# Loading the first keys in two parts, 16 rows ahead of the first query weights and 112 rows behind them

## The chip, the cores and the metric

The kernel runs on one core of a Trainium2 chip. The metric is the device time of one execution in microseconds; lower is better. All times are of the same kernel program on the chip, and the time before is the median of three runs.

## What is computed

A decode step for 4 tokens of width 448: a layer norm, attention of 16 query heads over 8 key/value heads with the last 1024 positions of a cache (head width 256), an output projection with a residual, then a second block of layer norm, a dense layer of 1792 with GELU, and a dense layer back with a residual.

```python
B, Sq, D = 4, 1, 448;  Hq, Hkv, Sk, Dh = 16, 8, 4096, 256;  W = 1024
def A(x):      # x is already normed
    q = (x @ wq).reshape(B, Sq, Hq, Dh).transpose(0, 2, 1, 3)
    k = repeat(k_cache[:, :, Sk - W:], 2, axis=1); v = repeat(v_cache[:, :, Sk - W:], 2, axis=1)
    p = softmax(einsum("bhqd,bhkd->bhqk", q, k) * Dh ** -0.5)
    return einsum("bhqk,bhkd->bhqd", p, v).transpose(0, 2, 1, 3).reshape(B, Sq, Hq * Dh) @ wo
h = x + A(layernorm(x))
y = layernorm(layernorm(h))
out = h + gelu(y @ w1 + b1) @ w2 + b2
```

Everything is in float32. Some 88 MB have to be read, nearly all of it keys, values and weights that are used once.

## The kernel before, in words

The work is cut by key/value head, two heads to a stage. For each stage the queries of both heads come from `wq` (tile `pq`), the scores (`b_s`) from the keys, the softmax and a transpose give `pT`, and the values (`b_o`) and the output weights (`b_acc`) end the stage. At the end stands the dense block with `w1` and `w2`.

All loads are issued from SyncE (SP) on one queue, in the order of the code. They go into a ring of three large slots in SBUF (`slot(...)`, all called `slot` in the profile). The helper `load(t, at, src)` issues one DMA of 128 rows (one row for each of the 128 partitions) into columns of a slot, and `cut` names the parts. Keys, values and weights of neighbouring stages are laid out behind one another on the host, so that one DMA brings a mixture of them: the arrays `l1` to `l8`. A load waits on SP until the last reader of its slot is done; the first three slots need no such wait.

The first slot `t0` takes two loads. `wq0` has 1828 columns: the query weights of head 0 (`WEIGHTS`, 1792 columns), and x and the two bias vectors in column form (`COLUMNS`, 36 columns). `k0` has 9728 columns: the keys of head 0 (8192 columns) and three quarters of the query weights of head 1 (1536 columns). The last part of head 1's query weights comes in two small loads of 32 rows each into `wq1_last`. Then follow `l1`, `l2` and the rest.

On the engines, the layer norm of x comes first (`column_mean` on PE, which reads `xT` out of `wq0`), then the projection of head 0, then six transposes that spread x and the biases (`b_t<-ident,slot`); the projection of head 1 and the scores of head 0 wait for `k0`.

Each operation is recorded first; a wait is derived for each from the part of a tile that it reads or writes (`Machine._needs`, in granules of 4 partitions), and every DMA has a semaphore of its own, which is called `landed_` and a number. So a reader of a part that two DMAs wrote waits for both. All instructions carry line 75, that of the recording helper.

Of the kernel before, what the change touches and what calls it, by code (L numbers as in the profile page):

```python
# [24 lines left out]
HALF = CACHE // 2  # L25
WEIGHTS = 4 * D
SLOT = CACHE + 2 * WEIGHTS + HALF
COLUMNS = ND * B + 4 + 4 * 4
# [172 lines left out]
def block_kernel(nc, wq0, k0, wq1, l1, l2, l3, l4, l5, l6, l7, l8, k7, vo, v7, wo, w1, w2, out):  # L201
    real, nc = nc, Machine(nc)
# [18 lines left out]
    def slot(name):  # L221
        return ring.tile([P, SLOT], F32, tag="slot", name=name)

    def load(t, at, src, pieces=None):
        dst = t[:, at : at + src.shape[-1]]
        at = 0
        for n in pieces or (src.shape[-1],):
            nc.sync.dma_start(dst[:, at : at + n], src[:, at : at + n])
            at += n
        return dst  # L230

    def cut(t, sizes):
        parts, at = [], 0
        for n in sizes:
            parts.append(t[:, at : at + n])
            at += n
        return parts


    def wq_parts(y, t, last=None):  # L240
        parts = [(a, y[:, a, :], slice(0, 512), t[:, a * 512 : (a + 1) * 512]) for a in range(3)]
        if last is not None:
            return parts + [(3, y[:H, 3, :], slice(0, 512), last)]
        for i in range(2):
            parts.append((3, y[:, 3 + i, :], slice(i * 2 * P, (i + 1) * 2 * P), t[:, 3 * 512 :]))
        return parts
# [204 lines left out]


    t = slot("t0")
    wqt, xT, b2T, b1T = cut(load(t, 0, wq0), (WEIGHTS, ND * B, 4, 4 * 4))
    wqt = wq_parts(yT[0], wqt)
    xT = xT.rearrange("p (a b) -> p a b", a=ND)
    ka, kb, wqt1 = cut(load(t, WEIGHTS + COLUMNS, k0), (HALF, HALF, 3 * 512))
    for i in range(2):
        nc.sync.dma_start(
            wq1_last[i * Q : (i + 1) * Q, :], wq1[i].rearrange("e (p c) -> e p c", c=512)[:, :4, :]  # L460
# [44 lines left out]
    ka, kb, va = cut(load(slot("l1"), 0, l1), (HALF, HALF, HALF))  # L505
# [14 lines left out]
    wq_a, wq_b, ka, kb, k2 = cut(load(slot("l3"), 0, l3), (WEIGHTS, WEIGHTS, HALF, HALF, HALF))  # L520
# [16 lines left out]
    v, wo_a, wo_b, ka = cut(load(slot("l5"), 0, l5), (CACHE, WEIGHTS, WEIGHTS, HALF))  # L537
# [6 lines left out]
    kb, ka, k2 = cut(load(slot("l6"), 0, l6), (HALF, HALF, HALF))  # L544
# [14 lines left out]
    vb, wo_a, wo_b, ka, kb = cut(load(slot("l8"), 0, l8), (HALF, WEIGHTS, WEIGHTS, HALF, HALF))  # L559
# [249 lines left out]
```

## Time and profile before

| | us |
|---|---|
| median of 3 runs | 211.96 (211.85 to 212.13) |
| profiled execution, its own time | 211.87 |
| span from the first to the last instruction in it | 210.6 |
| PE busy | 139.0 |
| DVE busy | 28.8 |
| ACT busy | 14.4 |

The profiled execution lies 0.09 us below the median; 1.27 us of it lie outside the span. The DMA queue of SP moved 88.30 MB in 3392 packets. "SPq" in the profile's rows is the time that SP's queue takes to issue a DMA, not the transfer itself; "us to landing" is from the issue until all of its data is in place. A row that has `<-DMA slot<-k` in its brackets waited for a load of keys.

### The profile page before, as it was taken

The numbers are of one execution on the slowest core, as the hardware profiler recorded it, in microseconds if no ns is written. First come the engines' busy times: TensorE is split into PE (matmuls) and PEld (weight loads), VectorE is DVE, ScalarE is ACT, GpSimd is POOL, SyncE is SP. The second block draws the span as 40 slices with busy tenths as digits, with TensorE's granted clock in tenths as the row PEclk, the third lists the DMA queues.
The fourth block names the chain that finished last, engine by engine and source line by source line (L and its number), as shares of the span: only waits on it lengthen the run. The fifth ranks groups of instructions, "written<-read, shape, count | busy, mean of one in ns | idle before, by whom it ended". The sixth has DMA issues, their size and how long they took to land.

```text
span 210.6 us, 2206 instructions
## 1 busy us (share of the span) xinstructions
PE 139.0 (66%) x984; PEld 47.2 (22%) x984; DVE 28.8 (14%) x135; ACT 14.4 (7%) x34; POOL 5.0 (2%) x17
## 2 busy tenths in 40 slices
PE   0467759621971679198359775419806999888996
PEld 0420202200220223034012222102301233224332
DVE  7210101300020011013001104000100213012320
ACT  2010000200000010020000002000100002010311
POOL 5100000000000000000000000000000000000100
PEclk9999996996799559969967999757965899999999
DMA  7999999899999999999999999999999999999993
GB/s 296 429 399 473 448 492 389 386 436 507 398 398 410 531 389 410 410 519 398 413 411 448 481 398 425 434 470 398 434 411 442 416 428 429 425 407 439 424 409 138
DMA packets 3400, 88.42 MB, mean 420 GB/s; under 512 B 512, under 2 KB 768, under 8 KB 1344
## 3 DMA queue, kind: packets, MB, share of 16 engines
q1 hardware_dynamic: 3392, 88.30, 97.6%
q8 instruction: 7, 0.11, 0.2%
q14 instruction: 1, 0.01, 0.0%
HBM read 88.23 MB, written 0.07 MB: 419 GB/s over the span
## 4 chain that ended last, share of the span: by engine, by line
DMA 77%; PE 18%; SPq 2%; DVE 1%; issue 1%; ACT 0%
DMA slot<-l 64%; DMA slot<-w 14%; PE b_o L75 9%; PE b_s L75 4%; PE b_acc L75 3%; SPq L75 2%; PE b_m L75 1%; DVE oT L75 1%; DVE w_o L75 0%; PE b_t L75 0%; DVE o_u L75 0%; ACT o_u L75 0%; DVE o_res L75 0%
## 5 line engine op out<-in xcount | busy, mean ns | idle before, releaser
L75 PE MATMUL b_o<-slot,pT 128*32 128x512 f32 x224 | 33.6, 752 | 29.3 <-DMA slot<-l 28.5
L75 PE MATMUL b_s<-slot,qT 128*32 128x512 f32 x256 | 36.6, 722 | 10.4 <-DMA slot<-l 9.1
L75 PE MATMUL b_m<-slot,yT 128*32 128x512 f32 (+1 forms) x76 | 11.9, 734 | 11.5 <-DMA slot<-l 6.4
L75 PEld LDWEIGHTS b_o<-slot,pT 128*32 128x32 f32 x224 | 7.8, 132 | 51.4 <-DMA slot<-l 30.9
L75 PE MATMUL b_t<-idle 128*32 128x512 bf16 x64 | 18.1, 404 | 0.5 <-DVE pT L75 0.5
L75 PEld LDWEIGHTS b_s<-slot,qT 128*32 128x32 f32 x256 | 8.8, 128 | 35.9 <-issue 22.5
L75 ACT ACTIVATE o_p<-b_s,w_nm 128x512 f32<-128x512 f32 x8 | 5.4, 682 | 93.1 <-DVE w_nm L75 93.1
L75 DVE TENSOR_REDUCE w_mx<-b_s 128x1 f32<-128x512 f32 x8 | 5.5, 692 | 43.7 <-PE b_s L75 43.7
L75 DVE TENSOR_SCALAR w_o<-b_o,w_rec 128x512 f32<-128x512 f32 x4 | 3.0, 751 | 52.5 <-PE b_o L75 52.5
L75 PEld LDWEIGHTS b_m<-slot,yT 128*32 128x32 f32 x76 | 4.3, 142 | 17.9 <-DMA slot<-l 6.9
L75 PEld LDWEIGHTS b_t<-idle 128*32 128x32 bf16 x64 | 5.9, 100 | 10.3 <-issue 5.8
L75 DVE TENSOR_REDUCE w_sm<-b_m 128x32 f32<-128x128 f32 x4 | 1.2, 291 | 48.2 <-PE b_m L75 48.2
L75 PE MATMUL b_t<-ident,o_p 128*128 128x128 f32 x32 | 5.0, 285 | 4.0 <-ACT o_p L75 3.9
L75 PE MATMUL b_acc<-slot,oT 128*32 128x448 f32 x52 | 6.1, 545 | 1.9 <-DVE oT L75 1.9
L75 ACT COPY w_qs<-b_m 128x512 f32<-128x512 f32 x4 | 2.3, 584 | 60.8 <-PE b_m L75 60.8
L75 POOL TENSOR_TENSOR o_r<-w_ve,mhalf 128x1 f32<-128x1 f32 x2 | 1.1, 542 | 189.0 <-DVE w_ve L75 189.0
L75 PE MATMUL b_m<-ident,w_qs 128*128 128x128 f32 x16 | 3.5, 361 | 2.9 <-ACT w_qs L75 2.9
L75 PEld LDWEIGHTS b_t<-ident,o_p 128*128 128x128 f32 x32 | 3.4, 141 | 7.4 <-ACT o_p L75 7.4
L75 PE MATMUL b_m<-slot,mean 128*128 128x12 f32 (+1 forms) x4 | 1.1, 370 | 5.6 <-DMA slot<-wq 5.6
L75 PE MATMUL b_o<-slot,yT 128*32 128x512 f32 x10 | 4.6, 594 | 0.0
L75 PE MATMUL b_m<-ident,w_o 128*128 128x128 f32 x20 | 3.3, 286 | 1.8 <-DVE w_o L75 1.8
L75 DVE COPY pT<-b_t 128x16 f32<-128x16 f32 x32 | 3.3, 167 | 6.0 <-PE b_t L75 6.0
(94 smaller groups left out, 66.7 us busy)
## 6 DMA issues: line engine op xcount, KB each, us to landing
slot<-l SPq DMA_DIRECT2D x6, 7936.0 KB, 43.0
slot<-l SPq DMA_DIRECT2D x2, 6144.0 KB, 34.1
slot<-k SPq DMA_DIRECT2D x1, 4864.0 KB, 15.9
slot<-vo SPq DMA_DIRECT2D x1, 4544.0 KB, 33.1
slot<-k SPq DMA_DIRECT2D x1, 4096.0 KB, 43.5
slot<-v SPq DMA_DIRECT2D x1, 3072.0 KB, 19.0
slot<-w SPq DMA_DIRECT2D x1, 2240.0 KB, 28.6
slot<-w SPq DMA_DIRECT2D x1, 1792.0 KB, 34.0
```

What stands on the lines that cost most here:

```text
L75: self.machine.add(Op(self.name, lambda: getattr(issuer, what)(*args, **kwargs), outs, ins, what))
```

## The change

`k0` is no longer loaded as one DMA of 128 rows. Its first 16 rows (partitions 0 to 15, 38,912 bytes each) are issued as the very first DMA, ahead of `wq0`; the other 112 rows (partitions 16 to 127) follow behind `wq0`. The places of the data in the slot, the number of bytes, and all the work on the other engines stay as they were.

```diff
     t = slot("t0")
+    k0t = t[:, WEIGHTS + COLUMNS :][:, : k0.shape[-1]]
+    nc.sync.dma_start(k0t[:16], k0[:16])
     wqt, xT, b2T, b1T = cut(load(t, 0, wq0), (WEIGHTS, ND * B, 4, 4 * 4))
     wqt = wq_parts(yT[0], wqt)
     xT = xT.rearrange("p (a b) -> p a b", a=ND)
-    ka, kb, wqt1 = cut(load(t, WEIGHTS + COLUMNS, k0), (HALF, HALF, 3 * 512))
+    nc.sync.dma_start(k0t[16:], k0[16:])
+    ka, kb, wqt1 = cut(k0t, (HALF, HALF, 3 * 512))
     for i in range(2):
         nc.sync.dma_start(
             wq1_last[i * Q : (i + 1) * Q, :], wq1[i].rearrange("e (p c) -> e p c", c=512)[:, :4, :]
```

SP's queue begins like this before. `slot<-wq` is `wq0`, `slot<-k` the first keys `k0`, `wq_last` the small loads of head 1's last query weights, `slot<-l` the mixed loads `l1`, `l2` and on:

```order
L75 DMA slot<-wq 128x1828
L75 DMA slot<-k 128x9728
L75 DMA wq_last<-wq 32x1x512 x2
L75 DMA slot<-l 128x12288
L75 DMA slot<-l 128x15872 x4
```

And after:

```order
L75 DMA slot<-k 16x9728
L75 DMA slot<-wq 128x1828
L75 DMA slot<-k 112x9728
L75 DMA wq_last<-wq 32x1x512 x2
L75 DMA slot<-l 128x12288
```

The first 16 rows of the keys have moved to the head of the queue, and everything else stands one issue later.

On PE, whose instructions keep their order, the waits of the projection of head 1 change. Before, `landed_27` is all of `k0`, and 28 and 29 are the two loads of `wq_last`; after, 26 is the 16 rows, 28 the 112 rows, and 29 and 30 `wq_last`:

```order
-L75 MATMUL b_m<-slot,yT 32x512 [waits landed_27]
+L75 MATMUL b_m<-slot,yT 32x512 [waits landed_26,landed_28]
 L75 MATMUL b_m<-slot,yT 32x512 x2
-L75 MATMUL b_m<-wq_last,yT 32x512 [waits landed_28,landed_29]
+L75 MATMUL b_m<-wq_last,yT 32x512 [waits landed_29,landed_30]
```

The first of these matmuls waits for both parts of the keys.

## The prediction

> **What bounds the kernel now.** I read the page first: the share of the DMA engines over the span, the queues, and the chain that ended last.
>
> ```profile
> span 210.6 us, 2206 instructions
> PE 139.0 (66%) x984; PEld 47.2 (22%) x984; DVE 28.8 (14%) x135; ACT 14.4 (7%) x34; POOL 5.0 (2%) x17
> DMA  7999999899999999999999999999999999999993
> ...
> ## 3 DMA queue, kind: packets, MB, share of 16 engines
> q1 hardware_dynamic: 3392, 88.30, 97.6%
> ...
> DMA 77%; PE 18%; SPq 2%; DVE 1%; issue 1%; ACT 0%
> ```
>
> SP's one queue keeps 16 DMA engines busy for 97.6% of the span; PE works 66% of it. Next came the same by stretches, to see where the stream is short of its pace. The columns are the stretch, its length, the PE clock, the DMA share and GB/s.
>
> ```profile
> 1.50:1.75 0.25, 1.00 0.41 88
> ...
> 1.50:2.50 1.00, 1.00 0.73 139
> 2.50:3.00 0.50, 1.00 0.85 322
> 3.00:4.00 1.00, 1.00 0.96 402
> 5.00:205.00 200.00, 0.87 1.00 430
> ```
>
> From 5 to 205 us the stream stands at 430 GB/s with nothing to gain. One engine then moves 430/16 = 26.9 GB/s, and one row of the first keys (9728 x 4 = 38,912 B) takes it 1.45 us. Only the first load is slow: from 1.50 to 3.00 us 139 x 1.00 + 322 x 0.50 = 300 KB arrive, where 430 GB/s would bring 645 KB. That is 345 KB or 0.80 us short; the stretch to 1.75 us, with 88 GB/s, is the coming of the first bytes and takes 0.25 us of it, so about 0.55 us is lost while engines are at work.
>
> Then the start in order of time (start, length, engine, work, and in brackets the idle time and who ended it):
>
> ```profile
> 0.73 0.39 SPq L75 DMA_DIRECT2D slot<-wq  x1
> 1.18 0.41 SPq L75 DMA_DIRECT2D slot<-k  x1
> 1.64 1.55 SPq L75 DMA_DIRECT2D wq_last<-wq  x2
> 3.23 0.98 SPq L75 DMA_DIRECT2D slot<-l  x2
> ...
> 5.63 1.12 PE L75 MATMUL b_m<-slot,mean 128*128 128x12 f32 x4 [5.63 <-DMA slot<-wq]
> ...
> 12.25 1.54 PE L75 MATMUL b_t<-ident,slot 128*128 128x128 f32 x6
> ...
> 17.13 1.93 PE L75 MATMUL b_m<-slot,yT 128*32 128x512 f32 x6 [3.33 <-DMA slot<-k]
> ...
> 24.21 5.21 PE L75 MATMUL b_s<-slot,qT 128*32 128x512 f32 x28
> 31.71 1.93 PE L75 MATMUL b_s<-slot,qT 128*32 128x512 f32 x8 [2.28 <-DMA slot<-l]
> ```
>
> PE waits for wq0, then for the first keys, then for l1. What follows x ends at 12.25 + 1.54 = 13.79 us, and the keys release PE at 17.13: 3.33 us of cover. Last, who ends PE's waits and SP's, and the end:
>
> ```profile
> PE b_o L75 <- DMA slot<-l: 28.5, 4, 8.3
> PE b_s L75 <- DMA slot<-l: 9.1, 3, 4.5
> ...
> SPq L75 <- PE b_acc L75: 59.3, 3, 21.2
> ...
> slot<-l SPq DMA_DIRECT2D x6, 7936.0 KB, 43.0
> slot<-k SPq DMA_DIRECT2D x1, 4864.0 KB, 15.9
> ...
> slot<-wq SPq DMA_DIRECT2D x1, 914.0 KB, 4.8
> ...
> 170.03 28.60 DMA slot<-w
> 198.63 0.14 issue
> ...
> 208.97 0.35 SPq L75 DMA_DIRECT2D out<-o_res  x1
> ```
>
> SP waits up to 21.2 us for a free slot, but a load of 7936 KB lands 43.0 us after its issue, where 430 GB/s moves it in 18.9 us: more than a whole load stands ahead of it, so the stream never runs dry. Every landing, the w1 one at 198.63 us that starts the tail too, moves one for one with time lost or won in the stream's first 17 us. Nothing downstream gives it back.
>
> **The change, part by part.** The bytes are the same; of the 38,912 B rows, 16 (622,592 B) now stand ahead of wq0 on SP's queue and 112 behind it. One issue is added. By its neighbours (0.39 and 0.41 us) wq0 is issued some 0.45 us later, and so are the small wq_last loads, l1 and l2 behind it. That costs nothing while the engines have the 16 rows to move (1.45 us at the least); without that cover it would be 0.45 us. PE, ahead of head 1's projection, waits for two landings of keys in place of one; the 112 rows land last anyway, so the second wait costs 0.
>
> *The 16 rows.* No row shows a load into so few partitions. Every load at 430 GB/s covers all 128 partitions, 8 rows to each of 16 engines. If each of the 16 rows has an engine and a way into memory of its own, they take 1.45 us, which is their share of the stream: +0. If 16 neighbouring partitions take in only 16/128 of the pace, it is 8 rows in line, 11.6 us: +10.2 us. Between lie 2 and 4 rows in line (2.9 and 5.8 us). The nearest rows of the trace are all loads of 128 partitions, whose pace is what the memory takes over its whole width, and that speaks for the slow half: I take 5.8 us, 4 rows in line, +4.35 us. While this runs, wq0 stands behind it on each engine.
>
> [...]
>
> *The 112 rows.* 7 rows to each of 16 engines is 10.15 us, +0. If the memory is entered by 16 blocks of 8 partitions, 112 rows lie in 14 of them with 8 rows each: 11.6 us, +1.45. And 7 rows for an engine no longer match a block of 8, so two engines can meet in one block; if they did all the time it would be 20.3 us, +10.15. The slowest engine counts, since a landing needs all of them and each later load again gives each engine the same work. Between +1.45 and +10.15 I take the geometric middle, +3.8 us.
>
> *The slow first load.* Behind 16 long rows, whatever holds up the first rows of wq0 can pass while the engines move data. Up to the 0.55 us above can be won; a loss is excluded, as the stretch exists already. I take -0.55, the end that leaves this cost to the 16 rows alone.
>
> *x and wq0 land later*, by 5.8 - 0.55 = 5.25 us: PE starts at 10.9 instead of 5.63, and what follows x (8.16 us from 5.63 to 13.79) ends at 19.0. The keys, late by the whole sum of 7.6 us, release PE at 24.7. Cover 5.7 us, cost 0. The same 7.6 us moves l1 and all that follows.
>
> Sum: +4.35 + 3.8 - 0.55 = **+7.6 us**. The profiled execution took 211.87 us (span 210.6 and 1.27 around it), 0.09 below the median of 211.96; 211.96 + 7.6 = **219.6 us**.
>
> **The rivals.**
>
> *Faster: 16 rows are one row for each engine, at full pace.* They land at 1.45 us of stream time and hide the slow first load: 211.96 - 0.55 = 211.4 us. For it speaks that the lost time is there and that the pace is the same for rows of any length in the trace; PE's cover holds (x later by 0.9 us against 3.33). It decides where the 16 rows take under 1.45 + 0.55 = 2.0 us. Against it: no load of the trace brings rows of this length to less than the full width.
>
> *No change.* Either the slow stretch belongs to the first microseconds and not to wq0, and the 16 rows run into it instead (211.96 + 0); or an engine serves fixed partitions, so the change doesn't spread these rows at all: the few engines of partitions 0 to 15 do the same rows, first instead of later, with the same total. Then wq0 lands 5.8 us late, PE's work on x ends at 19.6, 2.5 us after the keys, and of the slack ahead of l1 (2.28 us) it takes nearly all: 212.0 to 212.2 us.
>
> *Slower by the 16 rows alone,* the 112 at pace: 211.96 + 4.35 - 0.55 = 215.8 us.
>
> *Much slower: the 112 rows are dealt out one by one,* so that 16 neighbouring partitions are always in work together: 7 x 5.8 = 40.6 us instead of 10.15, near 246 us. Nothing in the profile speaks for this order.
>
> **How the numbers follow.** The forecast (16 rows at a quarter of the pace, 112 rows in each other's way) has 0.45, its own range 217 to 222 us: from half the cost of the 112 rows to +6 for them. Slower by the 16 rows alone 0.18, much slower 0.05, faster 0.22, no change 0.10. A measurement of this kernel tells 0.2%, 0.42 us, from no change; 211.4 is just beyond it. Slower is 0.45 + 0.18 + 0.05 = 0.68. The range goes from 211.2, to take in the faster case, to 222; the upper ends together (+20 us, 232) and the 246 stay out with the cases beyond.
>
> **What would show it.** In the profile after, the 608 KB load lands some 7 us after its issue (faster case: near 3); the first PE work starts near 10.9 us (6.5); PE's wait for the keys ends near 24.7 us (16.6), and that for l1 near 39.3 us (31.2). The 430 GB/s of the long middle stays as it is. In the first 8 us the forecast wants a stretch near a quarter of the pace. The forecast is wrong if the 16 rows land within 3 us of issue, or if the first keys land late and l1 does not.

## The result, and the profile after

The changed kernel takes 222.93 us (median of 4, 222.70 to 223.47) against 211.93 us (a fourth run is added to the three of 211.96): 11.0 us or 5.2% slower, ratio 1.0521 with a 95% interval of 1.0501 to 1.0542. The forecast was 219.6 us with a range of 211.2 to 222.0: the direction was right, the size was missed by 3.3 us, and the time lies 0.9 us above the upper end of the range. The profiled execution took 222.94 us, its span 221.4.

First the page of the profile after, the lines that answer to those of before:

```profile
span 221.4 us, 2208 instructions
PE 139.6 (63%) x984; PEld 47.8 (22%) x984; DVE 28.8 (13%) x135; ACT 14.4 (6%) x34; POOL 5.0 (2%) x17
...
GB/s 112 282 274 281 258 436 435 426 450 413 460 413 447 447 390 439 459 390 447 470 399 435 426 430 427 482 402 447 447 413 392 429 437 440 412 405 430 435 412 145
...
q1 hardware_dynamic: 3408, 88.30, 97.8%
```

The work of every engine is what it was, and the same 88.30 MB come in. The five first slices of 5.5 us each stand at 112 to 282 GB/s; all later ones but the last are back near 430. The DMA engines count as busy all the while (97.8%): the time is lost inside the transfers, not between them. That is easy to miss, since the busy share alone looks as good as before. The trace also keeps a record of every DMA packet (start, duration, bytes), and each of these rows of 38,912 B is one packet. Before, the 128 rows took 1.44 us each on average. After, the 16 rows all start between 1.75 and 2.31 us and take 3.7 to 5.4 us each; the 112 rows take 2.39 us on average, and none of them less than 1.67.

The issues of the first loads (KB, and us from issue to landing), and PE's waits for them in order of time:

```profile
slot<-k SPq DMA_DIRECT2D x1, 608.0 KB, 7.5
...
slot<-wq SPq DMA_DIRECT2D x1, 914.0 KB, 9.4
...
slot<-k SPq DMA_DIRECT2D x1, 4256.0 KB, 26.8
```

```profile
10.64 1.12 PE L75 MATMUL b_m<-slot,mean 128*128 128x12 f32 x4 [10.64 <-DMA slot<-wq]
...
28.47 1.93 PE L75 MATMUL b_m<-slot,yT 128*32 128x512 f32 x6 [9.79 <-DMA slot<-k]
...
43.01 3.64 PE L75 MATMUL b_s<-slot,qT 128*32 128x512 f32 x32 [2.60 <-DMA slot<-l]
```

wq0 releases PE at 10.64 instead of 5.63 us, 5.0 later; the keys at 28.47 instead of 17.13, 11.3 later; l1 at 43.01 instead of 31.71, 11.3 later. Of the first 5.0 us, 1.45 are the bytes of the 16 rows, which the stream had to move in any case. So 3.6 us are lost by the time that wq0 is in, another 7.8 by the time that the 112 rows are in, and nothing after. The chain of waits shows the same shift at the start of the tail:

```profile
180.79 28.56 DMA slot<-w
209.35 0.14 issue
```

209.35 instead of 198.63 us: 10.7 us, and the tail adds no more than 0.3.

### The profile page after: what moved, and what is told of

Same layout as the page of the kernel before. It is cut to its first block, busy times and chain, and to the rows that moved or that the text cites. A ratio compares the mean times of both kernels' runs of the same rounds, so it can differ in the third digit from the quotient of the medians.

```text
span 221.4 us, 2208 instructions
## 1 busy us (share of the span) xinstructions
PE 139.6 (63%) x984; PEld 47.8 (22%) x984; DVE 28.8 (13%) x135; ACT 14.4 (6%) x34; POOL 5.0 (2%) x17
## 3 DMA queue, kind: packets, MB, share of 16 engines
q1 hardware_dynamic: 3408, 88.30, 97.8%
## 4 chain that ended last, share of the span: by engine, by line
DMA 70%; PE 21%; another core or an unknown queue 4%; SPq 2%; DVE 2%; issue 1%; ACT 1%
DMA slot<-l 57%; DMA slot<-w 13%; PE b_o L75 10%; PE b_s L75 5%; PE b_acc L75 3%; SPq L75 2%; PE b_t L75 2%; PE b_m L75 1%; DVE oT L75 0%; ACT o_p L75 0%; DVE w_o L75 0%; DVE w_mx L75 0%; DVE o_u L75 0%; ACT o_u L75 0%
## 5 line engine op out<-in xcount | busy, mean ns | idle before, releaser
L75 PE MATMUL b_o<-slot,pT 128*32 128x512 f32 x224 | 34.1, 765 | 28.6 <-DMA slot<-l 27.7
L75 PE MATMUL b_s<-slot,qT 128*32 128x512 f32 x256 | 37.9, 746 | 9.4 <-DMA slot<-l 8.0
L75 PE MATMUL b_t<-idle 128*32 128x512 bf16 x64 | 16.8, 380 | 0.5 <-DVE pT L75 0.5
```

The lines of the kernel that those rows point to most:

```text
L75: self.machine.add(Op(self.name, lambda: getattr(issuer, what)(*args, **kwargs), outs, ins, what))
```

## The experiments

Theory A: rows in the wrong partitions at one time get in each other's way in the receiving memory. Theory B: few rows are slow wherever they go. Theory C: the 16 rows cost only their bytes. Others are named where they come up. The time before was 211.9 to 212.0 us beside each group of runs. The times are medians of 4 runs, of f4 and g4 of 11; durations of packets are those of one profiled execution of each kernel.

**What 16 rows cost by themselves.** The kernel before got an additional first DMA of 622,592 B, always the same number of bytes, into a slot whose own load comes later and overwrites them. The partitions differ, and with them the rows of `k0` that are read, since row p of the source always goes to partition p:

```diff
     t = slot("t0")
+    t1 = slot("l1")
+    nc.sync.dma_start(t1[:, :1216], k0[:, :1216])            # e1: all 128 partitions
+    nc.sync.dma_start(t1[:16, :9728], k0[:16])               # e2: 0 to 15
+    nc.sync.dma_start(t1[::8, :9728], k0[::8])               # e3: 0, 8 to 120
+    nc.sync.dma_start(t1[:106:7, :9728], k0[:106:7])         # e4: 0, 7 to 105
+    nc.sync.dma_start(t1[32:93:4, :9728], k0[32:93:4])       # f1: 32, 36 to 92
+    nc.sync.dma_start(t1[11:117:7, :9728], k0[11:117:7])     # f2: 11, 18 to 116
+    nc.sync.dma_start(t1[32:96, :2432], k0[32:96, :2432])    # f3: 32 to 95
+    nc.sync.dma_start(t1[:64, :2432], k0[:64, :2432])        # g3: 0 to 63
...
-    ka, kb, va = cut(load(slot("l1"), 0, l1), (HALF, HALF, HALF))
+    ka, kb, va = cut(load(t1, 0, l1), (HALF, HALF, HALF))
```

(one of the eight lines in each kernel). What was expected of the first four:

> The kernel before, with 622,592 B more loaded as the very first DMA: 1216 columns of all 128 partitions, into columns of the second slot that its own load overwrites later. All three theories: at the 430 GB/s of the long middle these bytes take 1.45 us, so about 213.4 us; down to 212.8 if the slow start (0.55 us short in the trace before) goes with them, up to 213.6. It is the price of the bytes alone, for the next three runs, which load as many bytes in 16 rows.

> The same extra bytes as 16 rows in partitions 0 to 15. In the changed kernel's trace the same 16 rows land 7.5 us after their issue, and wq0 was ready 5.0 us later than before (10.64 against 5.63 us). Theory A (rows in neighbouring partitions get in each other's way in the receiving memory): 5.0 us over before, 216.9 us. Theory B (few rows are slow wherever they go): 216.9 us too. Theory C (the rows cost their bytes, and it was the 112 rows that cost the 11 us): 213.4 us.

> The same, as 16 rows in partitions 0, 8, 16 to 120. Theory A: clearly less than with neighbours, between 212.8 and 215.5 us. Theory B: 216.9 us as with neighbours. Theory C: 213.4 us. [...]

> The same, as 16 rows in partitions 0, 7, 14 to 105. Theory A: no more than with every 8th, 212.8 to 215.5 us. Theory B: 216.9 us. Theory C: 213.4 us. [...]

And of the others:

> Again the kernel before with 622,592 B more as its first DMA, in 16 rows of 38,912 B, now in partitions 32, 36 to 92. Every 8th cost 215.25 us, every 7th 214.80, neighbours 216.93, the same bytes over all partitions 213.71. Theory A with fixed groups of partitions (the way into memory is shared by some partitions, and by which ones decides, not how far apart they lie): these 16 lie closer together than every 7th or 8th and can still be as fast as the full width, 213.3 to 213.9 us. Theory A with plain distance (the closer together, the slower): 215.25 to 216.9 us. [...]

> The same rows in partitions 11, 18 to 116, the spacing of the run with every 7th (214.80 us) shifted by 11. Theory A with fixed groups: a shift alone can change the time, down to 213.7 us. Theory A with plain distance: 214.8 us. Theory G (an engine is slow outside the partitions that it has in a 128-row load): at least 214.8 us, while partitions 32, 36 to 92 may be fast. [...]

> The same extra bytes as 64 neighbouring rows of 2432 columns, in partitions 32 to 95. The two halves (0 to 63 and 64 to 127) ran at half the pace, 208 GB/s. Theory A with fixed groups: the middle can differ from the halves, down to 213.7 us. Theory A with plain distance, or any theory in which the number of rows or partitions decides: as a half, 1.45 us over 213.7, about 215.2 us. [...]

> The control of the run with 64 rows in partitions 32 to 95 (214.06 us): the same 622,592 B as 64 rows of 2432 columns in partitions 0 to 63. Theory A with fixed groups: half the pace, 1.1 to 1.45 us more than the middle, 215.2 to 215.5 us. If the middle was fast only because so small a load is always fast: 214.06 us.

| run | partitions | us | over e1 | ratio to before (95%) |
|---|---|---|---|---|
| e1 | all 128 | 213.71 | | 1.0080 (1.0063 to 1.0097) |
| e2 | 0 to 15 | 216.93 | 3.22 | 1.0233 (1.0217 to 1.0248) |
| e3 | every 8th from 0 | 215.25 | 1.54 | 1.0153 (1.0138 to 1.0168) |
| e4 | every 7th from 0 | 214.80 | 1.09 | 1.0130 (1.0115 to 1.0145) |
| f1 | every 4th from 32 | 214.06 | 0.35 | 1.0101 (1.0088 to 1.0115) |
| f2 | every 7th from 11 | 214.25 | 0.54 | 1.0121 (1.0105 to 1.0137) |
| f3 | 32 to 95 | 214.06 | 0.35 | 1.0101 (1.0088 to 1.0115) |
| g3 | 0 to 63 | 215.26 | 1.55 | 1.0154 (1.0141 to 1.0168) |

The issues of e2, and below them those of f1, show the same difference at its source:

```profile
slot<-k SPq DMA_DIRECT2D x1, 608.0 KB, 7.6
```

```profile
slot<-k SPq DMA_DIRECT2D x1, 608.0 KB, 4.8
```

Same bytes, 16 rows each, same place in the queue: 2.8 us apart only by which rows and partitions they are. Theory B falls (16 rows go from 214.06 to 216.93 us), C falls with e2. The 16 packets of each run are all under way at once; one takes 4.5 us on average in e2, 2.8 in e3, 2.5 in e4, 2.3 in f1 and 2.1 in f2. By the times alone f2 and e4 can't be told apart, as their intervals overlap. Plain distance falls with f1 and f3: rows 4 apart from 32 on are faster than rows 8 apart from 0 on, and 64 neighbours are 1.20 us faster from 32 on than from 0 on. Of the theories that leaves A with fixed groups of partitions. Which partitions would form such a group is not shown. Nor did any run hold the source rows and move only the partitions, so that the conflict is on the receiving side is the author's inference. f1, f2 and f3 still cost 0.35 to 0.54 us more than e1; for f1 theory A with fixed groups had given 213.9 us at most. e1 itself cost 1.70 us over before where its bytes make 1.45.

e3 and g3 cost the same, 1.54 and 1.55 us over e1, although their rows and partitions are quite different ones; why is not shown.

**Eight rows at a time.** Four loads into 8 partitions each, ahead of wq0, each waiting for the one before; then the kernel as before (one execution, 232.3 us).

```diff
     t = slot("t0")
+    nc.sync.dma_start(t[0:29:4, :9728], k0[0:29:4, :9728])
+    nc.sync.dma_start(t[4:33:4, :9600], k0[4:33:4, :9600])
+    nc.sync.dma_start(t[0:36:5, :9472], k0[0:36:5, :9472])
+    nc.sync.dma_start(t[0:8, :9344], k0[0:8, :9344])
```

> Not for its time: four loads of 8 rows one after the other ahead of wq0, each waiting for the one before, each of about 38 KB a row, told apart by their size. 304 KB to partitions 0, 4 to 28; 300 KB to 4, 8 to 32; 296 KB to 0, 5 to 35; 292 KB to 0 to 7. Time from issue to landing with a row at 1.45 us and some 1.4 us of start and end: 2.8 us where nothing is in the way. Theory A (the partitions' ways into memory): 2.8, 2.8, then 2.8 to 4.2 us, and 4.2 to 7.2 us for 0 to 7. Theory B (few rows are slow): four times the same. Theory G (an engine is slow on any partition not its own): the second is slower than the first. [...]

The chain that ended last, from each issue to the landing that releases the next (start, length):

```profile
0.74 4.18 DMA slot<-k
4.92 0.02 issue
4.93 4.08 DMA slot<-k
9.01 0.02 issue
9.03 4.68 DMA slot<-k
13.71 0.02 issue
13.72 7.21 DMA slot<-k
```

4.18 and 4.08 us for the first two, 2.7 us more than the 1.45 us of a row at full pace, where 1.4 were expected; by the packet records most of their rows were slow too, up to 2.3 us. Rows shifted by 4 partitions cost no more (theory G falls). The last, 0 to 7, takes 3.1 us more than the second, and its rows 3.1 to 4.8 us each: 8 rows in neighbouring partitions are slower than 8 rows in partitions 4 apart, though their bytes are 2.7% fewer. The third, every 5th from 0 to 35, costs 0.5 to 0.6 us more than the first two, less than the 1.45 us of a whole row in line. Which of its rows hold each other up, if any, is not shown: the trace doesn't name the partition of a packet.

**The same keys, cut or laid out otherwise.** The 4.98 MB of the first keys behind wq0 in three ways: e5 as 16 and 112 rows, e6 as 64 and 64, e7 as one load of 128 rows, whose source is laid out in 16 groups of 8 rows with a gap behind each. Whether that changes which engine gets which row is not shown, as the trace doesn't name the engine of a packet.

```diff
-    ka, kb, wqt1 = cut(load(t, WEIGHTS + COLUMNS, k0), (HALF, HALF, 3 * 512))
+    k0t = t[:, WEIGHTS + COLUMNS :][:, : k0.shape[-1]]       # e7: [:, : 9728]
+    nc.sync.dma_start(k0t[0:16], k0[0:16])                   # e5
+    nc.sync.dma_start(k0t[16:128], k0[16:128])               # e5
+    nc.sync.dma_start(k0t[0:64], k0[0:64])                   # e6
+    nc.sync.dma_start(k0t[64:128], k0[64:128])               # e6
+    nc.sync.dma_start(k0t, k0.rearrange("e (p c) -> e p c", c=9728)[:, :8, :])    # e7
+    ka, kb, wqt1 = cut(k0t, (HALF, HALF, 3 * 512))
...
-    k0 = np.concatenate([k[0], wq[1][:, : 3 * 512]], axis=1)
+    k0 = np.concatenate([k[0], wq[1][:, : 3 * 512]], axis=1).reshape(16, 8 * 9728)  # e7
+    k0 = np.concatenate([k0, np.zeros((16, 9728), np.float32)], axis=1)             # e7
```

> Both parts of the keys behind wq0: wq0, 16 rows, 112 rows. The extra runs gave 3.2 us for the 16 neighbouring rows over their bytes (216.93 against 213.71), so of the 11.0 us of the change 7.8 us are left for the 112 rows. Theory A (rows in the wrong partitions at one time): order doesn't matter, 222.9 us (222 to 223.5), with PE's first work back at 5.6 us. Theory D (the 11 us come from x and wq0 being late): 212 us.

> The keys behind wq0 as 64 and 64 rows. Theory A: a half reaches fewer ways into memory than all 128 rows; if half of them, 4 rows of each engine take 2 x 4 x 1.45 = 11.6 us for each half, 23.2 us in all instead of 11.6, so 223.5 us. Theory E (only a count of rows that isn't a power of two, as 112, is dealt out badly): 212 us. Rows dealt as in one load of 128: 212 us. [...]

> [...] Bytes, rows, count and places are those of before. Theory A in the form that it matters which engine gets which partition: slower, up to 2 x 11.6 us for the load, 215 to 224 us. Theory F (only the number of rows or partitions of a load matters): 212 us, as before.

e6 takes 224.62 us (ratio 1.0606, 1.0584 to 1.0629) and e7 224.45 us (1.0590, 1.0574 to 1.0605), both somewhat more than theory A gave. GB/s in a stretch of the keys (stretch, its length, PE clock, DMA share, GB/s) of e6, of e7, and of the kernel before:

```profile
6.00:28.00 22.00, 1.00 0.96 199
```

```profile
6.00:28.00 22.00, 1.00 0.97 201
```

```profile
6.00:16.00 10.00, 1.00 0.97 418
```

Half the pace at the same busy share. e7 is the clearest run of all: bytes, rows, partitions and count are those of the load before, and it is 12.5 us slower. Nothing but the layout of the source differs: its rows take 2.95 us each on average instead of 1.44. It isn't the number of rows (theory F falls, and E with e6). Theory A explains it if the layout changes which rows are under way together. That it does, and that the kernel's own 128-row load is quick because its rows keep out of each other's way, is the author's inference and not shown.

e5 takes 225.23 us (ratio 1.0619, 1.0601 to 1.0636): theory D falls, as x is early (PE starts at 6.92 us) and the time is no better. But it is 2.3 us slower than the change, where theory A expected the same time. The landing of the load ahead is touched too:

```profile
slot<-wq SPq DMA_DIRECT2D x1, 914.0 KB, 6.1
...
slot<-k SPq DMA_DIRECT2D x1, 608.0 KB, 11.6
```

wq0, first in the queue and issued as before, lands 6.1 us after its issue instead of 4.8. Its last packet of data ends at 5.2 us in both traces, so the 1.3 us pass between the last packet and the landing; why is not shown. Most of the 2.3 us lies further on: the 112 rows, now right behind the 16, take 2.70 us each on average where the change has 2.39, and at 7 rows an engine (112 / 16, an estimate) that makes 2.2 us.

**The 112 rows by themselves.** As the extra runs, with 2.49 MB: g1 over all partitions, g2 in 112 rows.

```diff
+    nc.sync.dma_start(t1[:, :4864], k0[:, :4864])        # g1
+    nc.sync.dma_start(t1[16:, :5560], k0[16:, :5560])    # g2
```

> The kernel before with 2.49 MB more as its first DMA: 4864 columns of all 128 rows. At 430 GB/s 5.8 us, so 217.8 to 218.2 us by every theory. It is the price of the bytes for the next run.

> The same 2.49 MB as 112 rows of 5560 columns, in partitions 16 to 127, ahead of wq0. In the changed kernel, with 7.8 us for 4.36 MB, the 112 rows cost 77% on top of their 10.1 us. Theory H (every load of 112 rows dealt in sevens is slow by itself): 77% of 5.8 us, 4.5 us over the run before it, 222 to 223 us. Theory I (most of it came from the 16 rows ahead, which had put the engines out of step): 0 to 1.5 us over it, 218 to 219.5 us.

g1 takes 217.94 us (1.0282, 1.0266 to 1.0297), g2 221.12 us (1.0431, 1.0415 to 1.0446). The extra load of g1, and that of g2:

```profile
slot<-k SPq DMA_DIRECT2D x1, 2432.0 KB, 8.3
```

```profile
slot<-k SPq DMA_DIRECT2D x1, 2432.5 KB, 11.9
```

112 rows cost 3.18 us over 128 rows with the same bytes, 55% of their 5.8 us. That lies between the two theories: they are slow by themselves, but with 55% of 10.15 us, 5.6 us (scaled by the bytes, an estimate), not with all of the 7.8 that the change leaves for them (11.0 less 3.22). The packets account for more. In the change a row of the 112 took 2.39 us on average instead of 1.44, 66% more, which makes 6.7 us for 7 rows an engine (112 / 16, an estimate). In g2 it took 1.33 us where its 22,240 B make 0.83 at 26.9 GB/s (430 / 16, an estimate), 61% more. g2 less g1 is smaller because the rows of g1, first in the queue too, were slow as well (0.80 us, where their 19,456 B make 0.72). So the 112 rows are nearly as slow alone as in the change; of the 7.8 us about 1.1 stay open.

**Keys ahead, cut the other way.** f4 puts the same 622,592 B ahead of wq0 as columns of all 128 rows; g4 puts all of the first keys ahead.

```diff
     t = slot("t0")
+    k0t = t[:, WEIGHTS + COLUMNS :][:, : k0.shape[-1]]
+    nc.sync.dma_start(k0t[:, :1216], k0[:, :1216])       # f4
+    nc.sync.dma_start(k0t, k0)                           # g4
...
-    ka, kb, wqt1 = cut(load(t, WEIGHTS + COLUMNS, k0), (HALF, HALF, 3 * 512))
+    nc.sync.dma_start(k0t[:, 1216:], k0[:, 1216:])       # f4
+    ka, kb, wqt1 = cut(k0t, (HALF, HALF, 3 * 512))
```

> The change with another cut: the same 622,592 B of keys go ahead of wq0, as 1216 columns of all 128 rows, and the other 8512 columns behind it. Theory A: 212 us give or take 0.4, since all 128 partitions take part; PE starts 1.45 us later, at 7 us, inside its cover of 3.3 us. It was the cut by rows that cost, not keys ahead of wq0. If the slow start can be hidden behind keys, 211.4 us. Theory D (x and wq0 being late costs): slower by about 1.5 us.

> The first keys go ahead of wq0 whole, as one load of 128 rows. It asks whether the slow start can be hidden behind long rows over the full width, the term of -0.55 us in the prediction. If it can: 211.4 to 211.7 us. If the slow start is there whatever comes first: 211.9 to 212.3 us. x and wq0 land at about 17 us instead of 5.6; PE's work on x (8.2 us) then ends near 25.5 us, some 8 us later than it is needed now, against 2.3 us of slack ahead of l1 and 8.3 ahead of l2. If that cover is too thin: over 213 us.

Both take 212.30 us, ratio 1.0017 (f4 1.0009 to 1.0026, g4 1.0008 to 1.0026): 0.4 us slower, not 11. Keys ahead of wq0 were harmless here when all 128 partitions took part, and there is nothing to win by them either. That g4 loses no more shows how much cover the start has; its PE waits:

```profile
17.75 1.12 PE L75 MATMUL b_m<-slot,mean 128*128 128x12 f32 x4 [17.75 <-DMA slot<-wq]
52.41 6.69 PE L75 MATMUL b_o<-slot,pT 128*32 128x512 f32 x48 [6.51 <-DMA slot<-l]
```

x comes 12.1 us later than before, PE has no wait for the keys or l1 any more, and still waits 6.51 us for l2. No run beat the kernel before.

## Why the prediction was wrong in size

- *What bounds the kernel* was right: the stream is the bound from end to end. All of the loss arises in the first 28 us and passes through nearly one for one (keys +11.3, l1 +11.3, tail +10.7, run +11.0 us).
- *The 16 rows* were right in kind (16 neighbours are slower than 16 rows elsewhere, 216.93 us in e2 against 214.06 in f1), and near in size only together with the start: 4.35 - 0.55 = 3.8 us forecast, 3.22 measured between e2 and e1. That the marks came as forecast (landing 7.5 us after issue for some 7, PE's first work at 10.64 us for 10.9) is in part luck: the rows took 3.7 to 5.4 us and not the 5.8 of four in line, and from the issue to the first packet and from the last packet to the landing it was 2.1 us, where 1.2 had been assumed.
- *The 112 rows* are the step that failed: that they can cost more than their bytes was foreseen, the size was not. The geometric middle of +1.45 and +10.15 gave 3.8 us; g2 against g1 gives 5.6 us for them alone, their packets in the change 6.7, and the change leaves 7.8. That is more than the whole miss of 3.3 us; the other terms took 0.6 of it back. The marks say the same: the keys were forecast for 24.7 us and came at 28.47. The blocks of 8 partitions behind these bounds were a supposition that no run shows, and no row of the profile stood behind the choice of the geometric middle; the plain middle of the bounds, 5.8 us, would have been nearer, though still too low. The term also took the 112 rows as if it didn't matter what stands ahead of them, and e5 against the change shows that it does. The range left the time out, as 222 allowed 6 us for this term.
- *The slow first load* was not to be had where loads over the full width stood ahead of wq0: e1, f4 and g4 show 0.25 to 0.4 us of loss, which the prediction excluded, in place of the 0.55 us of gain. Behind the 16 rows this term can't be told from theirs. Why the first load is slow is not shown.
- *x and wq0 late* cost nothing, as forecast; e5 and g4 confirm it from both sides.
- *The rivals.* The faster case fell at the point that it named: it needed the 16 rows in under 2.0 us of stream time, and they cost 4.9 with their bytes (e2 over before). That an engine serves fixed partitions, so that nothing is lost in all, fell with the time and with the trace after: 16 rows for a few engines would start one behind another, and all 16 start within 0.6 us. The 16 rows alone would have been 215.8 us; the 112 rows were not at pace. Nor did they come near the 246 us of rows dealt out one by one.

## What to carry to other kernels

In these runs the pace of a load hung on which rows it had for which partitions: the same 0.62 MB in 64 rows cost 215.26 us from partition 0 on and 214.06 us from 32 on. So where a load of 128 rows has to be cut, cut it by columns: f4 cost 0.4 us where the same bytes cut by rows cost 11.0. If rows must be cut, choose which (for 0.62 MB, every 4th partition from 32, or 32 to 95, were nearly as good as all 128), and price both pieces, since here the larger, harmless-looking one cost more. And a DMA share of 97% doesn't mean full pace: read GB/s beside it.

## What the runs showed that was not expected

The same 128 rows cost 12.5 us more when their source was laid out in 16 groups of 8 with a gap behind each (e7). Loading 16 rows and then all 128 of them again elsewhere (e2, 216.93 us) is 6.0 us faster than loading 16 and the missing 112 (222.93 us), although it moves 0.62 MB more. And the 16 rows touched their neighbours in the queue: in e5 wq0 ahead of it landed 1.3 us later, and the 112 rows behind it took 2.70 us each instead of 2.39.
